# A step's fourth and fifth product exchanged, and the weight sets of the second layer re-timed, in a two-layer kernel planned at build time

## The chip, the core and the metric

The kernel runs on one core of one Trainium2 chip. The metric is the device time of one execution in microseconds (us). One more execution was recorded by the hardware profiler, and the views below are of that one.

## What is computed

The reference is a linear attention whose output feeds two dense feed-forward layers, all in fp32:

```
kv  = einsum('bhsd,bhse->bhde', k, v);  out = einsum('bhsd,bhde->bhse', q, kv)
a   = out / sqrt(mean(out*out, -1) + 1e-6) * g_norm          # 8 x 8 x 576 x 64
x   = a, heads side by side                                  # 4608 tokens x 512
x   = (s * relu(x @ w_in)**2 + b) @ w_out                    # first layer, 512 -> 2048 -> 512
out = silu(x @ w_in2) @ w_out2                               # second layer
```

## The kernel before

**Precision.** TensorE multiplies in a reduced fp32 form. Each fp32 factor is split into a rounded part and a rest, and each product is three matmuls (high by high, high by rest, rest by high), always 128x128 by 128x512.

**Stages.** The tokens are nine blocks of 512. The attention makes all blocks, and meanwhile the first layer works through blocks 0 to 4 one at a time, in 80 units (`unit`, 16 per block; the first matmuls stand at lines L210 to L212). Then come six pairs of blocks, 0 to 5 (`hidden`, `outputs`): pairs 0 and 1 are the first layer on the last four blocks, pairs 2 to 5 the second layer on eight blocks. One last block ends the second layer in units again.

**A pair's step.** A pair uses Strassen's scheme in Winograd's form, with seven products for eight. `hidden(tp, j)` is step j (of 8) of pair tp: the seven products B11, T2, T1, B21, T3, T4, B22 in that order, each in two halves of three matmuls (L964). They accumulate in three PSUM banks, X, Y and Z: `BANK = (X, Y, Z, X, Y, Y, Z)`. VectorE (DVE) takes the sums between them: `x1` copies X after B11; `u2` = Y + x1 is read after T2; `u3` = Y + x1 after T3; then `h22` = Z + u3. All of u2, u3 and h22 stand at L989. Three of them free a bank for a product: T3 may not start before u2 is read, T4 not before u3, B22 not before h22. `outputs` multiplies two finished steps by the second weight matrix (L1098 to L1100, six matmuls each), `total` takes each result from PSUM into a tile `ya`, and `results` adds those up on GpSimd (POOL, L1132) and stores them.

**Sets.** Each weight matrix of a layer is cut in 8 sets of two 128-row tiles; a set is turned into the 8 Winograd factors (`factors`) and stored in DRAM. There are 32 sets, 16 per layer. A set of the second layer is 4 loads, the decoding of a wide number format on ScalarE (ACT), DVE and POOL, 4 sums, 8 splits and 8 stores, about 60 short instructions on DVE, ACT, POOL and the DMA queue. Decoded tiles come from a pool of SBUF that is closed after the last set; only then are four more buffers for the pairs' inputs (`Q_RING`) and two for hidden values there (`turn3`).

**Order.** Nobody writes the order by hand. Every operation goes to `Plan.add` with a key, its needs, and a price per engine; `Plan.run` simulates the engines and emits each operation when and where it would start first, among equals the lowest key. What it emits is each engine's fixed order on the chip, and every engine works through its order strictly in turn. All DMAs are issued by SyncE (SP). The plan prices a DMA at 0.7 us to start, its transfer (0.73 us for 256 KB), and 1.1 us to end.

Of the kernel before, what the change touches and what calls it, by code (L numbers as in the profile page):

```python
# [19 lines left out]
class Plan:  # L20
# [112 lines left out]
def kernel(  # L133
# [237 lines left out]
    def factors(layer, kind, j, key, before):  # L371
        me = (layer, kind, j)
        begin = [started(key)] + (before or [("w", 0, k_, m, 1) for k_, m in late])
        b = [("rq", me + (n,)) for n in range(8)]
        w = lambda n: w32[b[n]][:, 1]
        full = lambda n: [("full", n) + me]
        for f in range(2):
            for c in range(2):
                n, m = quarter_of(kind, f, c), 2 * j + f
                if layer:  # L380
                    decode(1, kind, m, c, QW, "2", key + 0.2 * (2 * f + c), needs=begin, quarter=b[n], made=full(n))
# [499 lines left out]
    def pair_direct(tp):  # L881
# [16 lines left out]
        for kk in range(KH):  # L898
# [44 lines left out]
    def hidden(tp, j):  # L943
# [63 lines left out]
        S = lambda n: lambda: tmp[n, me]  # L1007
        add({ACT: 0.59, DVE: 0.69}, k(0), x1, needs=done(0), makes=[("x1",) + me], takes=[tb["x1"]])
        add({DVE: 0.69}, k(1), plus("u", Y, "x1"), needs=done(1) + [("x1",) + me], makes=[("u2",) + me], takes=[tb["u"]])
        add({DVE: 0.69}, k(4), plus("b", Y, "x1"), needs=done(4) + [("u2",) + me] + turn_, makes=[("u3",) + me], takes=[tb["b"]])  # L1010
        add({DVE: 0.69}, k(4) + 0.05, plus("b", Z, "b"), needs=done(2) + [("u3",) + me], makes=[("h22",) + me])
        add({DVE: 0.69}, k(5), add_up("c", B(Y), S("x1"), ALU.add), needs=done(5) + [("u3",) + me], makes=[("h21",) + me],
            gives=[tb["x1"]])
        add({DVE: 0.69}, k(6), add_up("a", B(Z), S("u"), ALU.add), needs=done(6) + [("h22",) + me], makes=[("h12",) + me],
            gives=[tb["u"]])

        for src, ready, kk in (("d", done(3) + [("x1",) + me], k(3)), ("b", [("h22",) + me], k(4) + 0.1),
                               ("c", [("h21",) + me], k(5) + 0.1), ("a", [("h12",) + me], k(6) + 0.1)):
            def curve(e, src=src):
# [334 lines left out]
```

## Time and profile before

| | us |
|---|---|
| median of 3 runs | 1608.47 (1605.17 to 1610.91) |
| the profiled execution, its own time | 1607.83 |
| its span, first to last instruction | 1606.1 |
| TensorE (PE) busy in the span | 1568.3 (98%) |
| VectorE (DVE) busy | 1069.5 (67%) |
| ScalarE (ACT) busy | 925.2 (58%) |
| GpSimd (POOL) busy | 627.0 (39%) |

Busy time is the union of an engine's instructions. A matmul's end is modelled and overlaps the next, so a stretch in which PE is fully busy says only that it never stood still. The number of matmuls that it began in a stretch tells more.

### The profile page before, as it was taken

The numbers are of one execution on the slowest core, as the hardware profiler recorded it, in microseconds if no ns is written. First come the engines' busy times: TensorE is split into PE (matmuls) and PEld (weight loads), VectorE is DVE, ScalarE is ACT, GpSimd is POOL, SyncE is SP. The second block draws the span as 40 slices with busy tenths as digits, with TensorE's granted clock in tenths as the row PEclk, the third lists the DMA queues.
The fourth block names the chain that finished last, engine by engine and source line by source line (L and its number), as shares of the span: only waits on it lengthen the run. The fifth ranks groups of instructions, "written<-read, shape, count | busy, mean of one in ns | idle before, by whom it ended". The sixth has DMA issues, their size and how long they took to land.

```text
span 1606.1 us, 23369 instructions
## 1 busy us (share of the span) xinstructions
PE 1568.3 (98%) x7393; PEld 1263.6 (79%) x7393; DVE 1069.5 (67%) x1944; ACT 925.2 (58%) x1791; POOL 627.0 (39%) x566
## 2 busy tenths in 40 slices
PE   8999999999999999999999999999999999999999
PEld 6777877877777777787788888888888788878887
DVE  6786777777776577988678746765667566656521
ACT  5896666666677677776667453544354445444222
POOL 1331111211225133457637752762266237622310
PEclk9999999999999999999999999999999999999999
DMA  9765687886666889888878786777687767876684
GB/s 217 187 177 149 209 262 238 253 236 207 194 221 210 281 274 301 290 259 276 276 243 260 254 267 192 242 213 233 187 285 197 238 190 239 198 230 192 206 205 140
DMA packets 354395, 366.49 MB, mean 228 GB/s; under 512 B 175712, under 2 KB 237152, under 8 KB 354272
## 3 DMA queue, kind: packets, MB, share of 16 engines
q1 hardware_dynamic: 354144, 365.00, 75.5%
q8 instruction: 59, 0.97, 0.2%
q14 instruction: 64, 0.52, 0.1%
q0 software_dynamic: 128, 0.00, 0.0%
HBM read 274.73 MB, written 90.18 MB: 227 GB/s over the span
## 4 chain that ended last, share of the span: by engine, by line
PE 49%; DMA 4%; DVE 2%; SPq 2%; POOL 1%; issue 1%; ACT 0%; DVEq 0%; POOLq 0%; ACTq 0%
PE hp L964 21%; PE acc L1098 8%; PE acc L1100 8%; PE acc L1099 7%; SPq L227 2%; DMA win<-wi 1%; PE acc L773 1%; PE acc L771 1%; PE acc L772 1%; PE h L210 1%; PE h L212 1%; PE h L211 1%; POOL ya L1132 1%; DMA xt_d<-ya 0%; DMA x<-x_d 0%
## 5 line engine op out<-in xcount | busy, mean ns | idle before, releaser
L964 PE MATMUL hp<-xo,win 128*128 128x512 f32 x2016 | 516.8, 393 | 12.8 <-DVE tmp L989 10.4
L964 PEld LDWEIGHTS hp<-xo,win 128*128 128x128 f32 x2016 | 378.7, 188 | 103.6 <-DVE tmp L989 15.1
L218 POOL TENSOR_TENSOR g<-tmp,g 128x512 fp32r<-128x512 f32 x192 | 249.8, 1304 | 358.2 <-ACT g L215 253.1
L1098 PE MATMUL acc<-g,wout 128*128 128x512 f32 x672 | 265.2, 395 | 2.1 <-DVE ya L224 1.3
L1107 DVE TENSOR_TENSOR ya<-acc,ya 128x512 f32<-128x512 f32 x252 | 172.2, 686 | 140.3 <-PE acc L1100 134.5
L1100 PE MATMUL acc<-g,wout 128*128 128x512 f32 x672 | 264.0, 393 | 0.0
L1099 PE MATMUL acc<-g,wout 128*128 128x512 f32 x672 | 263.3, 392 | 0.0
L1098 PEld LDWEIGHTS acc<-g,wout 128*128 128x128 f32 x672 | 126.4, 188 | 31.1 <-DVE ya L224 1.7
L1100 PEld LDWEIGHTS acc<-g,wout 128*128 128x128 f32 x672 | 126.5, 188 | 29.0
L1099 PEld LDWEIGHTS acc<-g,wout 128*128 128x128 f32 x672 | 126.4, 188 | 27.1 <-POOL g L218 0.2
L210 PE MATMUL acc<-gh,wo 128*128 128x512 f32 x320 | 133.6, 418 | 1.4 <-ACT gh L215 1.4
L215 ACT ACTIVATE g<-tmp 128x512 fp32r<-128x512 f32 x192 | 121.0, 630 | 24.1 <-DVE tmp L1003 16.3
L211 PE MATMUL acc<-gh,wo 128*128 128x512 f32 x320 | 127.4, 398 | 3.5 <-DVE gh L218 3.5
L210 PE MATMUL h<-xh,wi 128*128 128x512 f32 x320 | 126.8, 396 | 0.5 <-DVE gh L218 0.5
L212 PE MATMUL acc<-gh,wo 128*128 128x512 f32 x320 | 126.2, 394 | 0.1
L212 PE MATMUL h<-xh,wi 128*128 128x512 f32 x320 | 125.2, 391 | 0.0
L211 PE MATMUL h<-xl,wi 128*128 128x512 f32 x320 | 124.9, 390 | 0.0
L734 ACT ACTIVATE h<-h 128x512 f32<-128x512 f32 x96 | 55.9, 582 | 119.0 <-PE h L212 118.5
L215 ACT ACTIVATE g<-hp 128x512 fp32r<-128x512 f32 x144 | 85.9, 596 | 66.8 <-PE acc L1100 30.4
L989 DVE TENSOR_TENSOR tmp<-hp,tmp 128x512 f32<-128x512 f32 x144 | 98.6, 685 | 38.3 <-PE hp L964 35.5
L218 DVE TENSOR_TENSOR g<-hp,g 128x512 fp32r<-128x512 f32 x144 | 98.6, 685 | 34.7 <-ACT g L215 34.2
L1003 DVE TENSOR_TENSOR hp<-hp,tmp 128x512 f32<-128x512 f32 x144 | 99.6, 694 | 31.6 <-PE hp L964 30.9
(147 smaller groups left out, 2604.6 us busy)
## 6 DMA issues: line engine op xcount, KB each, us to landing
wout<-wo SPq DMA_DIRECT2D x368, 256.0 KB, 3.9
win<-wi SPq DMA_DIRECT2D x144, 512.0 KB, 5.0
wi<-rq SPq DMA_DIRECT2D x96, 256.0 KB, 3.2
wo<-rq SPq DMA_DIRECT2D x96, 256.0 KB, 3.5
win<-wi SPq DMA_DIRECT2D x80, 256.0 KB, 4.0
raw<-in_moe_w_out_dram SPq DMA_DIRECT2D x38, 256.0 KB, 4.4
raw<-in_moe_w_in_dram SPq DMA_DIRECT2D x34, 256.0 KB, 4.0
q<-in_q_dram SPq DMA_DIRECT2D x112, 72.0 KB, 2.9
```

What stands on the lines that cost most here:

```text
L210: nc.tensor.matmul(ps, wh, xh, start=first, stop=False)
L211: nc.tensor.matmul(ps, wh, xl, start=False, stop=False)
L212: nc.tensor.matmul(ps, wl, xh, start=False, stop=last)
L215: nc.scalar.activation(hi, src, AF.Copy)
L218: eng[e].tensor_tensor(lo, src, f32(hi), op=ALU.subtract)
L964: nc.tensor.matmul(to, w[:, wn, f_], x_[:, xn], start=first and n == 0, stop=kk == KH - 1 and n == 2, skip_group_check=True)
L989: nc.vector.tensor_tensor(t, bank[me, a], tmp[b_, me], op=ALU.add)
L1003: nc.vector.tensor_tensor(t, a(), b_(), op=op)
L1098: nc.tensor.matmul(to, w[:, 0, dd], gh, start=a == 0, stop=False)
L1099: nc.tensor.matmul(to, w[:, 0, dd], gl, start=False, stop=False)
L1100: nc.tensor.matmul(to, w[:, 1, dd], gh, start=False, stop=a == 1)
L1107: nc.vector.tensor_tensor(y2[tp, i, d], st["ps"], y2[tp, i, d], op=ALU.add)
```

## The change

Three things change. T3 and B21 change places in the order of the products (with the factors that they use, A12 and S3, which are stored in that order), so that T3 is the fourth product and B21 the fifth. The second layer's sets get other keys: 8 of them instead of 12 have keys ahead of the pairs, and those in the pairs get keys 6 units later. And after 100 us of planned time the plan prices a DMA's transfer 10% longer and its end at 1.6 us.

```
-    DMA_START, DMA_END = 0.7, 1.1
+    DMA_START, DMA_END, DMA_BUSY, BUSY_FROM, BUSY_RATE = 0.7, 1.1, 1.6, 100, 1.1
...
-                dma = max(dma, end + self.DMA_START) + op[8]
-                end = dma + self.DMA_END
+                busy = end > self.BUSY_FROM
+                dma = max(dma, end + self.DMA_START) + op[8] * (self.BUSY_RATE if busy else 1.0)
+                end = dma + (self.DMA_BUSY if busy else self.DMA_END)
...
-    A11, S2, S1, A12, S3, A22, S4, A21 = range(8)
+    A11, S2, S1, S3, A12, A22, S4, A21 = range(8)
...
+        late_key = key + (6 if key >= base(0) - 6 else 0)
...
-            k2 = key + 0.7 + 0.05 * n
+            k2 = late_key + 0.7 + 0.05 * n
...
-    B11, T2, T1, B21, T3, T4, B22 = range(7)
+    B11, T2, T1, T3, B21, T4, B22 = range(7)
...
-    BANK = (X, Y, Z, X, Y, Y, Z)
+    BANK = (X, Y, Z, Y, X, Y, Z)
...
-        read = {3: "x1", 4: "u2", 5: "u3", 6: "h22"}
+        read = {B21: "x1", T3: "u2", T4: "u3", B22: "h22"}
...
-        add({DVE: 0.69}, k(4), plus("b", Y, "x1"), needs=done(4) + [("u2",) + me] + turn_, makes=[("u3",) + me], takes=[tb["b"]])
+        add({DVE: 0.69}, k(T3), plus("b", Y, "x1"), needs=done(T3) + [("u2",) + me] + turn_, makes=[("u3",) + me], takes=[tb["b"]])
...
-        steps = ((0, KF + 3), (2 * NS, 48), (2 * NS + 12, base(0) - 6), (len(sets), base(NL1) + 8))
+        steps = ((0, KF + 3), (2 * NS, 44), (2 * NS + 8, base(0) - 6), (len(sets), base(NL1) + 8))
```

Since the plan is made anew, instructions move on every engine from about the 14th unit on. Three places follow; lines of the changed kernel are numbered up to two higher.

**PE, end of step 0 of pair 0.** In a name such as `xo31` the first digit is the product's place in the step, the second its half; `hp` is a bank, and `acc` belongs to the last unit. Before:

```order
L964 MATMUL hp_6440<-xo21_5810,win_5998 128x512 x3
L210 MATMUL acc_5644<-gh_6393,wo15_1833 128x512
L211 MATMUL acc_5644<-gh_6394,wo15_1833 128x512
L212 MATMUL acc_5644<-gh_6393,wo15_1833 128x512
L964 MATMUL hp_6375<-xo30_5756,win_5998 128x512 x3
L964 MATMUL hp_6375<-xo31_5863,win_5998 128x512 x3
L964 MATMUL hp_6404<-xo40_5779,win_6047 128x512 x3
L964 MATMUL hp_6404<-xo41_5877,win_6047 128x512 x3
L964 MATMUL hp_6404<-xo50_5915,win_6047 128x512 x3
L964 MATMUL hp_6404<-xo51_5964,win_6047 128x512 x3
L964 MATMUL hp_6440<-xo60_5953,win_6053 128x512 x3
```

And now:

```order
L966 MATMUL hp_6418<-xo21_5889,win_5993 128x512 x3
L211 MATMUL acc_5648<-gh_6372,wo15_1869 128x512
L212 MATMUL acc_5648<-gh_6373,wo15_1869 128x512
L213 MATMUL acc_5648<-gh_6372,wo15_1869 128x512
L966 MATMUL hp_6385<-xo30_5720,win_5993 128x512 x3
L966 MATMUL hp_6385<-xo31_5856,win_5993 128x512 x3
L966 MATMUL hp_6354<-xo40_5785,win_6047 128x512 x3
L966 MATMUL hp_6354<-xo41_5872,win_6047 128x512 x3
L966 MATMUL hp_6385<-xo50_6000,win_6047 128x512 x3
L966 MATMUL hp_6385<-xo51_6032,win_6047 128x512 x3
L966 MATMUL hp_6418<-xo60_6039,win_6054 128x512 x3
```

Before, the fifth and the sixth product (T3, T4) follow each other in bank Y (`hp_6404`); now B21's six matmuls in X (`hp_6354`) stand between them, and between T2 and T3 only T1 is left.

**DVE, the same step, from u2 (the first L989 row) to h22 (the last).** The rows between belong to sets, but for L224, which is a block's output. Before:

```order
L989 TENSOR_TENSOR tmp_6437<-hp_6404,tmp_6401 128x512
L320 TENSOR_SCALAR raw_6414<-raw_6414 128x256
L305 TENSOR_SCALAR raw_6414<-raw_6414 128x256
L320 TENSOR_SCALAR raw_6420<-raw_6420 128x256
...
L403 TENSOR_TENSOR rq_6479<-rq_6389,rq_6455 128x256
L403 TENSOR_TENSOR rq_6486<-rq_6479,rq_6384 128x256
L218 TENSOR_TENSOR rq_6455<-rq_6455 128x256
L218 TENSOR_TENSOR rq_6384<-rq_6384 128x256
L218 TENSOR_TENSOR rq_6479<-rq_6479 128x256
L218 TENSOR_TENSOR rq_6389<-rq_6389 128x256
L989 TENSOR_TENSOR tmp_6503<-hp_6404,tmp_6401 128x512
L989 TENSOR_TENSOR tmp_6503<-hp_6440,tmp_6503 128x512
```

And now:

```order
L991 TENSOR_TENSOR tmp_6415<-hp_6385,tmp_6382 128x512
L225 COPY y_6424<-acc_5616 128x512
L306 TENSOR_SCALAR raw_6380<-raw_6380 128x256
L321 TENSOR_SCALAR raw_6380<-raw_6380 128x256
L311 SCALAR_TENSOR_TENSOR raw_6380<-rq_6422,raw_6380 128x256
L321 TENSOR_SCALAR raw_6406<-raw_6406 128x256
L991 TENSOR_TENSOR tmp_6457<-hp_6385,tmp_6382 128x512
L306 TENSOR_SCALAR raw_6406<-raw_6406 128x256
L991 TENSOR_TENSOR tmp_6457<-hp_6418,tmp_6457 128x512
```

Twelve rows of a set stood between u2 and u3; now four do, and one output.

**SP, the loads of pair 4, step 3.** `win` is a load of first weights (the row of interest is its third group), `wout` one of second weights, `out` a store of pair 3's results. Before:

```order
L227 DMA out_0_dram<-ya_7056 32x16x32 x4
L227 DMA wout_12945<-wo2_0_103 128x512
L227 DMA wout_12945<-wo2_1_104 128x512
L227 DMA out_0_dram<-ya_6973 32x16x32 x4
L227 DMA win_12976<-wi2_3_98 128x1024
```

And now:

```order
L228 DMA win_12830<-wi2_3_98 128x1024
L228 DMA wout_12836<-wo2_0_103 128x512
L228 DMA wout_12836<-wo2_1_104 128x512
L228 DMA out_0_dram<-ya_6869 32x16x32 x4
L228 DMA win_12870<-wi2_3_98 128x1024
L228 DMA out_0_dram<-ya_6668 32x16x32 x4
```

The third group of `win` was issued behind all eight stores of the pair before it; now it is issued behind three. Pairs 3 and 5 show the same.

## Rows read from the trace of the kernel before

**Rows 1.** The page's first lines: span, and PE's busy time.

```profile
span 1606.1 us, 23369 instructions
PE 1568.3 (98%) x7393; PEld 1263.6 (79%) x7393; DVE 1069.5 (67%) x1944; ACT 925.2 (58%) x1791; POOL 627.0 (39%) x566
```

**Rows 2.** Windows: each engine's busy us (and instructions begun), clock, DMA share.

```profile
450.00:550.00 100.00, 95.93 (x412) 75.89 (x411) 68.56 (x140) 71.52 (x146) 34.85 (x38) 1.00 0.72 238
550.00:600.00 50.00, 45.88 (x189) 35.97 (x188) 36.37 (x86) 38.56 (x79) 14.65 (x17) 0.97 0.74 242
600.00:650.00 50.00, 47.62 (x204) 37.46 (x203) 38.36 (x83) 38.11 (x77) 18.25 (x19) 1.00 0.91 302
650.00:700.00 50.00, 48.48 (x211) 39.27 (x210) 45.03 (x85) 36.91 (x71) 21.60 (x21) 1.00 0.87 287
700.00:750.00 50.00, 47.40 (x199) 37.96 (x198) 40.96 (x70) 36.46 (x67) 33.82 (x29) 0.97 0.80 253
750.00:800.00 50.00, 47.67 (x207) 38.28 (x206) 33.31 (x49) 34.37 (x60) 38.88 (x31) 1.00 0.89 291
800.00:850.00 50.00, 49.62 (x218) 40.44 (x217) 36.34 (x66) 31.66 (x59) 20.64 (x21) 1.00 0.78 249
850.00:900.00 50.00, 49.94 (x219) 40.63 (x218) 43.27 (x63) 35.39 (x62) 38.41 (x29) 1.00 0.83 264
1300.00:1400.00 100.00, 100.00 (x437) 81.73 (x436) 66.97 (x104) 47.29 (x82) 60.90 (x48) 1.00 0.75 212
```

**Rows 3.** What PE waited for: us in total, times, longest.

```profile
PE hp L964 <- DVE tmp L989: 10.4, 9, 2.4
PE hp L964 <- DMA win<-wi: 1.7, 3, 0.7
```

**Rows 4.** Timeline of PE: four starts of T4, with the wait before each.

```profile
575.32 5.05 PE L964 MATMUL hp<-xo,win 128*128 128x512 f32 x14 [2.16 <-DVE tmp L989]
...
588.02 1.65 PE L964 MATMUL hp<-xo,win 128*128 128x512 f32 x6 [1.29 <-DVE tmp L989]
...
771.10 1.20 PE L964 MATMUL hp<-xo,win 128*128 128x512 f32 x4 [1.27 <-DVE tmp L989]
...
791.86 1.43 PE L964 MATMUL hp<-xo,win 128*128 128x512 f32 x5 [1.06 <-DVE tmp L989]
```

**Rows 5.** Timeline of DVE up to the u3 that the first of these waited for.

```profile
572.09 0.42 DVE L403 TENSOR_TENSOR rq<-rq 128x256 f32<-128x256 f32 x1 [0.78 <-POOL rq L324]
572.90 0.42 DVE L403 TENSOR_TENSOR rq<-rq 128x256 f32<-128x256 f32 x1 [0.38 <-DMA wo<-rq]
573.24 1.43 DVE L218 TENSOR_TENSOR rq<-rq 128x256 fp32r<-128x256 f32 x4
574.58 1.41 DVE L989 TENSOR_TENSOR tmp<-hp,tmp 128x512 f32<-128x512 f32 x2
```

**Rows 6.** Windows behind two of PE's waits: the clock stands before the DMA share.

```profile
575.40:578.80 3.40, 3.40 (x8) 2.65 (x9) 1.61 (x3) 2.67 (x5) 1.56 (x2) 0.51 1.01 377
725.60:729.00 3.40, 3.40 (x10) 2.66 (x9) 2.71 (x6) 1.96 (x5) 2.66 (x3) 0.50 0.58 192
```

**Rows 7.** Timeline of PE: the last start before, and T3 of pair 1, step 0.

```profile
718.76 3.83 PE L964 MATMUL hp<-xo,win 128*128 128x512 f32 x15
725.02 1.16 PE L964 MATMUL hp<-xo,win 128*128 128x512 f32 x3 [2.43 <-DVE tmp L989]
```

**Rows 8.** Timeline of DVE: first and last of nine instructions ahead of that T3's u2, and u2.

```profile
719.15 0.68 DVE L1107 TENSOR_TENSOR ya<-acc,ya 128x512 f32<-128x512 f32 x1
...
723.69 0.69 DVE L1003 TENSOR_TENSOR hp<-hp,tmp 128x512 f32<-128x512 f32 x1
724.29 0.68 DVE L989 TENSOR_TENSOR tmp<-hp,tmp 128x512 f32<-128x512 f32 x1
```

**Rows 9.** DVE's sums of inputs in 565 to 900: ns, minimum, median, maximum.

```profile
L907 DVE TENSOR_TENSOR x<-x x6: 676/1026/1673, 711.2 to 877.4; 128x512 f32<-128x512 f32 x6
```

**Rows 10.** Timeline of PE: two waits in a run of outputs.

```profile
627.53 0.50 PE L1098 MATMUL acc<-g,wout 128*128 128x512 f32 x1 [1.27 <-DVE ya L224]
...
629.73 0.51 PE L1098 MATMUL acc<-g,wout 128*128 128x512 f32 x1 [0.54 <-ACT ya L222]
```

**Rows 11.** DMA issues in 700 to 870: KB each, median us to landing.

```profile
wout<-wo SPq DMA_DIRECT2D x59, 256.0 KB, 4.6
xt_d<-ya SPq DMA_DIRECT2D x8, 256.0 KB, 7.0
raw<-in_moe_w_out_dram SPq DMA_DIRECT2D x4, 256.0 KB, 4.5
```

**Rows 12.** Timeline of DVE: a copy held up by a store, and the u3 behind it.

```profile
790.52 0.69 DVE L224 COPY ya<-acc 128x512 f32<-128x512 f32 x1 [1.75 <-DMA xt_d<-ya]
791.12 0.68 DVE L989 TENSOR_TENSOR tmp<-hp,tmp 128x512 f32<-128x512 f32 x1
```

**Rows 13.** Pair 3, step 5: PE's row of T2's second half, and DVE up to u2.

```profile
1129.96 1.55 PE L964 MATMUL hp<-xo,win 128*128 128x512 f32 x6
...
1130.74 0.69 DVE L218 TENSOR_TENSOR g<-hp,g 128x512 fp32r<-128x512 f32 x1 [0.66 <-ACT g L215]
1131.35 0.69 DVE L1003 TENSOR_TENSOR hp<-hp,tmp 128x512 f32<-128x512 f32 x1
1131.95 0.68 DVE L1107 TENSOR_TENSOR ya<-acc,ya 128x512 f32<-128x512 f32 x1
1132.54 0.68 DVE L989 TENSOR_TENSOR tmp<-hp,tmp 128x512 f32<-128x512 f32 x1
```

More of the change, by code (lines that the diff above doesn't have):

```diff
@@ L380, in factors @@
                 if layer:
-                    decode(1, kind, m, c, QW, "2", key + 0.2 * (2 * f + c), needs=begin, quarter=b[n], made=full(n))
+                    decode(1, kind, m, c, QW, "2", late_key + 0.2 * (2 * f + c), needs=begin, quarter=b[n], made=full(n))
                     continue
@@ L392, in spill @@
                     dma(w_d[0, kind, j][:, n], f32(w_t[kind, 0, m])[:, :, cs])
-                add(both(QW), key + 0.05 * (2 * f + c), recover, needs=ready + begin, makes=full(n), takes=[b[n]],
+                add(both(QW), late_key + 0.05 * (2 * f + c), recover, needs=ready + begin, makes=full(n), takes=[b[n]],
                     gives=lent_to[f"w{kind}{m}"])
                 if n != A21:
-                    add({"SP": 0.48}, key + 0.4 + 0.05 * (2 * f + c), spill, needs=full(n), makes=[("wd", n) + me],
+                    add({"SP": 0.48}, late_key + 0.4 + 0.05 * (2 * f + c), spill, needs=full(n), makes=[("wd", n) + me],
                         gives=lent_to[f"w{kind}{m}"], move=0.73)
@@ L403, in go @@
                 eng[e].tensor_tensor(w(o), w(x), w(y), op=op)
-            add(both(QW), key + 0.6 + 0.01 * o, go, needs=full(x) + full(y), makes=full(o), takes=[b[o]],
+            add(both(QW), late_key + 0.6 + 0.01 * o, go, needs=full(x) + full(y), makes=full(o), takes=[b[o]],
                 gives=[] if layer else [b[n] for n in (x, y) if n not in (S1, S2)])
@@ L907, in go @@
                     eng[e].tensor_tensor(tile_[dst, kk], tile_[a, kk], tile_[b_, kk], op=op)
-                at = {T3: -3, T1: -2.5, T2: 4 / 7 * 0.8 - 1.2, T4: 4 / 7 * 3.8 - 1.2}[o]
+                at = {T3: -3, T1: -2.5, T2: 4 / 7 * 0.8 - 1.2, T4: 4 / 7 * 4.8 - 1.2}[o]
                 add(both(T), base(tp) + at + 0.3 * kk, go, needs=needs, makes=[sx(o)], gives=[x[n, kk] for n in gives])
@@ L1007, in hidden @@
         S = lambda n: lambda: tmp[n, me]
-        add({ACT: 0.59, DVE: 0.69}, k(0), x1, needs=done(0), makes=[("x1",) + me], takes=[tb["x1"]])
-        add({DVE: 0.69}, k(1), plus("u", Y, "x1"), needs=done(1) + [("x1",) + me], makes=[("u2",) + me], takes=[tb["u"]])
-        add({DVE: 0.69}, k(4), plus("b", Y, "x1"), needs=done(4) + [("u2",) + me] + turn_, makes=[("u3",) + me], takes=[tb["b"]])
-        add({DVE: 0.69}, k(4) + 0.05, plus("b", Z, "b"), needs=done(2) + [("u3",) + me], makes=[("h22",) + me])
-        add({DVE: 0.69}, k(5), add_up("c", B(Y), S("x1"), ALU.add), needs=done(5) + [("u3",) + me], makes=[("h21",) + me],
+        add({ACT: 0.59, DVE: 0.69}, k(B11), x1, needs=done(B11), makes=[("x1",) + me], takes=[tb["x1"]])
+        add({DVE: 0.69}, k(T2), plus("u", Y, "x1"), needs=done(T2) + [("x1",) + me], makes=[("u2",) + me], takes=[tb["u"]])
+        add({DVE: 0.69}, k(T3), plus("b", Y, "x1"), needs=done(T3) + [("u2",) + me] + turn_, makes=[("u3",) + me], takes=[tb["b"]])
+        add({DVE: 0.69}, k(T3) + 0.05, plus("b", Z, "b"), needs=done(T1) + [("u3",) + me], makes=[("h22",) + me])
+        add({DVE: 0.69}, k(T4), add_up("c", B(Y), S("x1"), ALU.add), needs=done(T4) + [("u3",) + me], makes=[("h21",) + me],
             gives=[tb["x1"]])
-        add({DVE: 0.69}, k(6), add_up("a", B(Z), S("u"), ALU.add), needs=done(6) + [("h22",) + me], makes=[("h12",) + me],
+        add({DVE: 0.69}, k(B22), add_up("a", B(Z), S("u"), ALU.add), needs=done(B22) + [("h22",) + me], makes=[("h12",) + me],
             gives=[tb["u"]])
-        for src, ready, kk in (("d", done(3) + [("x1",) + me], k(3)), ("b", [("h22",) + me], k(4) + 0.1),
-                               ("c", [("h21",) + me], k(5) + 0.1), ("a", [("h12",) + me], k(6) + 0.1)):
+        for src, ready, kk in (("d", done(B21) + [("x1",) + me], k(B21)), ("b", [("h22",) + me], k(T3) + 0.1),
+                               ("c", [("h21",) + me], k(T4) + 0.1), ("a", [("h12",) + me], k(B22) + 0.1)):
             def curve(e, src=src):
@@ L1042, in hidden @@
         for i, src, ready, kk, gives in (
-            (B11, "d", sg("d"), k(3) + 0.1, []), (B22, "b", sg("b"), k(4) + 0.2, []), (B21, "c", sg("c"), k(5) + 0.2, []),
+            (B11, "d", sg("d"), k(B21) + 0.1, []), (B22, "b", sg("b"), k(T3) + 0.2, []), (B21, "c", sg("c"), k(5) + 0.2, []),
             (T1, "e", sg("e"), kt + 0.03, [tb["e"]]), (T3, "a2", sg("a2"), kt + 0.05, []), (T2, "f", sg("f"), kt + 0.07, []),
```

## The prediction

> **What bounds the kernel now.** The page's first lines come first: PE is busy for 1568.3 of 1606.1 us, far ahead of DVE [rows 1]. So only a moment in which PE stands still, or runs below full speed, can be given back. How much that is at which stage is read from the windows, by counting matmuls: a fully fed stretch, 1300 to 1400, begins 437 in 100 us, that is 0.2288 us each [rows 2]. The six windows from 550 to 850, which hold the last units of the first layer and pairs 0 and 1, begin 189 + 204 + 211 + 199 + 207 + 218 = 1228, where 1311 fit: 83 x 0.2288 = 19.0 us are lost there. The window 450 to 550 begins 412 and loses 25 x 0.2288 = 5.7 us. From 850 on little is lost (219 of 218.5 in the next window). In both stretches DVE and ACT work on the second layer's sets beside the units and pairs.
>
> Next the list of waits: PE's waits at L964 on a `tmp` of L989 are 10.4 us in 9, and loads of `win` make it wait 1.7 us [rows 3]. The timeline of PE gives the places. Four starts of T4 wait 2.16, 1.29, 1.27 and 1.06 us [rows 4]; T3 of pair 1, step 0, waits 2.43 [rows 7]; two starts in a run of outputs wait 1.27 and 0.54 [rows 10]. Then DVE's timeline up to the value waited for: the u3 of the first T4 stands behind seven short instructions of sets, two of which wait themselves, for POOL and for a store [rows 5]; the u2 of the T3 stands behind nine instructions that run almost without a gap from 719.15 to 724.29 [rows 8]. A late u3 hits PE at once, since T4 follows T3 in the same bank with nothing of the step between. Last, the clock: right after the two long waits the granted clock is 0.51 and 0.50 for 3.4 us, the lower of the two levels (1.2 of 2.4 GHz) [rows 6]. At half speed 3.4 us do the work of 1.7, so each of these waits costs 1.7 us more.
>
> **The change part by part.** Gains first, then new waits.
>
> *T4 behind B21 instead of T3.* Six matmuls, 6 x 0.2288 = 1.37 us, now lie between T3's end and T4, and u3 can be taken in them. That covers the waits of 1.29, 1.27 and 1.06 by itself; even a copy held up 1.75 us by a store, after which the last of these came [rows 12], is then hidden. It covers 2.16 only to 0.8, but there the order also shows four set rows and one output ahead of u3 in place of twelve set rows. I take all: 2.16 + 1.29 + 1.27 + 1.06 = 5.8, and the first one's dip, 1.7: **7.5 removed**. Bound: the first keeps 0.8 us and its dip, 5.0.
>
> *T3 of pair 1, step 0.* The nine instructions ahead of u2 thin out, as outputs and sets are spread differently, and 2.43 + 1.7 = 4.1 go. But T3 now has only T1, 1.37 us, behind T2, and in the new order a sum of inputs stands right ahead of u2. Such a sum takes 0.68 to 1.67 us, 1.03 in the median [rows 9]; with one of 1.4 the sum is 0.21 for PE's end to be seen + 1.4 + 0.69 for u2 + 0.06 to release PE = 2.36, and 2.36 - 1.37 = 1.0 stays: **3.1 removed** (bounds 4.1, and nothing if the queue is as full as before).
>
> *The run of outputs.* 1.27 + 0.54: **1.8 removed**, since products of the next step now stand between them (bound nothing).
>
> *The rest of that stage.* 19.0 - 7.5 - 4.1 - 1.8 = 5.6 us are short waits on sets and their buffers. Fewer sets fall in the last units, but the work is only moved. I take half, **2.8 removed** (0 to 5.6).
>
> *450 to 550.* The 5.7 us lie where sets are made between units. About 3.5 sets end there now instead of about 5, by the order, so 5.7 x 1.5 / 5 = **1.7 removed** (0 to 5.7). The first layer's sets come up to four units earlier; nothing waits there in either list, so 0.
>
> *Loads of `win` in step 3 of pairs 3 to 5.* Issued ahead of five stores instead of behind all eight: **1.7 removed** [rows 3] (bound nothing).
>
> *The price of a DMA.* It costs no instruction. A 256 KB load is now planned to land after 0.7 + 0.73 x 1.1 + 1.6 = 3.1 us instead of 2.5. The trace says 4.5 and 4.6 for loads, and 7.0 for the stores `xt_d` that free a `ya` [rows 11]. So instructions that need a DMA are put later, though still earlier than it lands. By the Trainium skill ("DMA: Bandwidth & Descriptors", section "Anatomy of one DMA — SWDGE (gpsimd) path") a transfer, on GpSimd's path, takes about 2.0 us and its bytes over 436e9 a second, an estimate of 2.6 us for 256 KB. By that the new price would be long enough, and the 2.6 us of stores below would fall away; this trace, whose issues are SP's, disagrees [rows 11].
>
> *New waits, outputs.* In steps 4 of pairs 1 and 2 the new order has bunches of four to seven outputs, each of which needs a `ya`, and a `ya` is free when its store has landed: 7.0 us against 3.1 planned, 3.9 late at most. Before, such a copy waited 1.75 [rows 12]. I take 1.3 on PE each, like the 1.27 of [rows 10]: **2.6 added** (0 to 7.8).
>
> *New wait, start of pair 2.* Sets end later, so the four input buffers and two hidden ones opened behind them come in pair 2, step 2, instead of pair 1, step 6. Sums of inputs for pair 2, and ten outputs in step 0, meet POOL's share of the last sets. I take **2.0 added** (from nothing to 2.43 + 1.7 = 4.1, as at the worst start above). By the Trainium skill ("SBUF — State Buffer", section "SBUF: two separate sides") DVE with two SBUF operands and GpSimd share a pair of ports, and one waits for the whole instruction of the other. That speaks against more such work at a pair's start; the spread of 676 to 1673 ns for one form agrees [rows 9].
>
> *T3's halved cover.* In pairs 0 and 1, with irregular work on DVE, T3 has one product less behind T2 in all 16 steps. Three waits of 0.5 us, as the shortest of [rows 10]: **1.5 added** (0 to 16 x 0.5 = 8). In the second layer's steady steps it is closer: T2's second half begins at 1129.96, and u2, third of a run that starts when ACT's value comes, ends at 1132.54 + 0.68 = 1133.22, that is 3.26 later [rows 13]. T3 is now due 15 matmuls behind that half's start, 15 x 0.2288 = 3.43 us. Less 0.05 until PE goes on (724.29 + 0.68 to 725.02 [rows 7, 8]) 0.12 us are spare; cost 0. Without that cover it costs PE the whole excess in each of some 40 steps.
>
> Sum: 7.5 + 3.1 + 1.8 + 2.8 + 1.7 + 1.7 = 18.6 removed, 2.6 + 2.0 + 1.5 = 6.1 added, 12.5 net. The profiled execution took 1607.8, so 1595.3; it lies 0.6 below the median of the runs, so for a median **1596 us**.
>
> **The rivals.**
> *Nearly all goes.* The 5.6 and 5.7 leave too, and of the new waits only 2 to 4 us stay: 7.5 + 3.1 + 1.8 + 5.6 + 4 + 1.7 = 23.7, less 3, is 20.7: about **1587**. For it speaks that DVE is busy only 67% [rows 1]; against it that sets must still be made beside the pairs.
> *The sets are only pushed back.* The bunches wait their full 7.8, pair 2's start 4.1: 18.6 - 7.8 - 4.1 - 1.5 = 5.2, about **1603**. For it speaks the 7.0 [rows 11], against it that PE has hidden products planned between most outputs.
> *DVE's queue is as bad as before.* DMAs still land later than planned, so the head of DVE's queue waits [rows 5, 12] and only T4's 5.0 and the 1.7 of `win` go, with 4 us of new waits: 2.7, about **1605**, no measurable change.
> *u2 is not in time.* If one more DVE instruction (0.60 from start to start [rows 13]) gets ahead of u2 in the steady steps, T3 waits 0.60 - 0.12 = 0.48, 40 times, 19 us: 1595.9 + 19 = about **1615**, slower. It decides from 12.5 / 40 + 0.12 = 0.43 us of lateness in each step. Against it: the same three instructions stand ahead of u2, in the same sequence.
>
> **How the numbers follow.** Forecast (1590 to 1601) 0.52; nearly all 0.14; pushed back 0.14; queue as bad 0.11; u2 late 0.09. A change of 0.3%, 4.8 us, is about what a measurement of this kernel can tell, so 1603.6 to 1613.3 counts as the same: the queue case, half of pushed back and 0.02 of u2 late, 0.20. Slower is the rest of u2 late, 0.07; faster is what remains, 0.73. The range reaches from below the first rival, 1585, to just above the queue case, 1607; it leaves out u2 late and tails.
>
> **What would show it.** Right, if the windows from 550 to 850 begin some 1260 matmuls instead of 1228, no T4 waits over 0.3 us on L991, and the clock stays at 1.00 there but for pair 1's or pair 2's start. Each step by itself: `win` no longer among PE's waits; PE waiting on `ya` or `acc` in steps 4; L991 with small waits at T3 in pairs 0 and 1. Wrong, if T3 waits some tenths of a us in every second-layer step, or if PE's loss moves to 850 to 950, where it lost nothing.

## The result, and the profile after

The changed kernel takes 1588.68 us (median of 4 runs, 1588.18 to 1589.46); the kernel before took 1606.82 over 4 (one more than in the table above). The ratio is 0.9887, 95% interval 0.9860 to 0.9914: 18 us faster, and the span of the profiled execution fell by 18.8, from 1606.1 to 1587.3. The forecast was 1596, range 1585 to 1607.

The first lines of the page after, against [rows 1]:

```profile
span 1587.3 us, 23243 instructions
PE 1558.8 (98%) x7393; PEld 1263.9 (80%) x7393; DVE 1075.8 (68%) x1937; ACT 914.3 (58%) x1779; POOL 641.6 (40%) x585
```

PE has the same 7393 matmuls, and stood still less. Where, the windows tell, columns as in [rows 2]:

```profile
450.00:550.00 100.00, 99.11 (x434) 80.55 (x433) 63.96 (x133) 71.72 (x147) 32.69 (x34) 1.00 0.73 242
550.00:600.00 50.00, 46.88 (x198) 38.05 (x197) 33.44 (x63) 38.34 (x75) 18.70 (x19) 0.97 0.71 225
600.00:650.00 50.00, 50.00 (x221) 41.16 (x220) 41.23 (x73) 32.81 (x65) 20.73 (x22) 1.00 0.87 284
650.00:700.00 50.00, 50.00 (x220) 41.10 (x219) 41.54 (x68) 38.45 (x74) 31.13 (x29) 1.00 0.84 264
700.00:750.00 50.00, 49.06 (x214) 39.70 (x213) 42.29 (x71) 34.99 (x66) 39.84 (x34) 1.00 0.84 272
750.00:800.00 50.00, 44.91 (x187) 35.78 (x187) 37.38 (x64) 31.78 (x60) 31.45 (x28) 0.97 0.89 291
800.00:850.00 50.00, 50.00 (x221) 41.14 (x220) 41.43 (x76) 34.52 (x67) 25.77 (x26) 1.00 0.85 278
```

From 550 to 850 there are 1261 matmuls instead of 1228, and 450 to 550 has 434 instead of 412. But these windows don't show all of it: the same clock time is now about 11 us further on in the program. So the starts of the same matmul in both traces are compared:

| first matmul of | before, us | after, us | gained in the part up to it |
|---|---|---|---|
| pair 0 (attention and units done) | 561.2 | 550.4 | 10.8 |
| pair 2 (pairs 0 and 1 done) | 873.9 | 855.8 | 7.2 |
| pair 3 (pair 2 done) | 1028.2 | 1012.3 | -2.1 |
| the last units | 1493.7 | 1475.0 | 2.8 |

More than half of the gain came before pair 0, where the prediction had looked at 450 to 550 only. One window over the units shows it, first before, then after:

```profile
200.00:450.00 250.00, 244.13 (x1372) 194.83 (x1371) 179.47 (x405) 162.35 (x368) 45.10 (x60) 1.00 0.79 235
```

```profile
200.00:450.00 250.00, 249.08 (x1401) 200.46 (x1400) 187.85 (x428) 167.82 (x376) 51.10 (x67) 1.00 0.78 236
```

PE stood still for 5.9 us there and now does for 0.9. The waits of DVE in 195 to 450, again before and after, say what came in time:

```profile
DVE raw L320 <- DMA raw<-in_moe_w_in_dram: 7.2, 7, 2.3
DVE raw L320 <- DMA raw<-in_moe_w_out_dram: 5.0, 6, 1.8
```

```profile
DVE raw L321 <- DMA raw<-in_moe_w_out_dram: 1.5, 1, 1.5
DVE raw L321 <- DMA raw<-in_moe_w_in_dram: 1.2, 1, 1.2
```

`raw` is a set's tile as loaded. DVE stood with a decoding instruction at the head of its queue until the load had landed, 12.2 us in all; now 2.7. The list of PE's waits, against [rows 3], has these:

```profile
PE acc L1100 <- DVE ya L225: 5.0, 2, 3.6
PE hp L966 <- DVE g L219: 3.1, 1, 3.1
PE acc L1100 <- DVE ya L1109: 1.5, 2, 0.9
PE hp L966 <- DVE tmp L991: 0.9, 2, 0.6
```

The waits for a `tmp` fell from 10.4 to 0.9 and those for `win` are gone, but two of over 3 us are new. Behind both, the granted clock (it stands before the DMA share) is at the lower of its two levels for 3.4 us:

```profile
580.20:583.60 3.40, 3.40 (x10) 2.65 (x9) 2.47 (x5) 2.73 (x6) 0.86 (x2) 0.50 0.37 104
757.70:761.10 3.40, 3.40 (x10) 2.62 (x9) 0.76 (x2) 3.40 (x8) 2.71 (x3) 0.50 0.73 172
```

So the two falls of the clock that [rows 6] showed have not gone: there are two again, behind other waits. The first of these waits is at T2 of step 2 of pair 0:

```profile
579.06 3.26 PE L966 MATMUL hp<-xo,win 128*128 128x512 f32 x9 [3.12 <-DVE g L219]
```

T2 needs bank Y, which the step before gives back with its last `g`. Before, it waited 0.42 us there, after T4 had waited 2.16 and 1.29 in steps 0 and 1. Counted by matmuls, these three steps lost 6.5 us before and lose 5.0 now: most of what T4 lost there has moved, and has not gone.

The wait at 757 is worth following. PE's row, then DVE's timeline up to the `ya` that it waited for, then POOL's:

```profile
756.82 0.50 PE L1100 MATMUL acc<-g,wout 128*128 128x512 f32 x1 [3.62 <-DVE ya L225]
```

```profile
745.75 1.26 DVE L405 TENSOR_TENSOR rq<-rq 128x256 f32<-128x256 f32 x1
747.01 0.69 DVE L219 TENSOR_TENSOR g<-hp,g 128x512 fp32r<-128x512 f32 x1
747.62 0.83 DVE L405 TENSOR_TENSOR rq<-rq 128x256 f32<-128x256 f32 x1
748.37 7.20 DVE L219 TENSOR_TENSOR rq<-rq 128x256 fp32r<-128x256 f32 x5
755.49 0.69 DVE L1005 TENSOR_TENSOR hp<-hp,tmp 128x512 f32<-128x512 f32 x1
756.09 0.68 DVE L225 COPY ya<-acc 128x512 f32<-128x512 f32 x1
```

```profile
745.43 9.86 POOL L1134 TENSOR_TENSOR ya<-ya 128x512 f32<-128x512 f32 x7
```

Five splits of a set take 7.20 us, 1.43 us from start to start, where a split of this form takes 0.42 (the median of 34 from 600 on). Beside them POOL sums pair 0's results, seven in 9.86 us, 1.40 us from start to start, where the first alone takes 1.29. Both go forward in the same steps: they take turns. The `g` of 747.01, which has only one operand in SBUF (`hp` is a bank), takes its usual 0.69 us beside the same sums. The kernel before has such slow sums and splits too, 6 of over 0.9 us between 680 and 800, against 9 now.

### The profile page after: what moved, and what is told of

Same layout as the page of the kernel before. It is cut to its first block, busy times and chain, and to the rows that moved or that the text cites. A ratio compares the mean times of both kernels' runs of the same rounds, so it can differ in the third digit from the quotient of the medians.

```text
span 1587.3 us, 23243 instructions
## 1 busy us (share of the span) xinstructions
PE 1558.8 (98%) x7393; PEld 1263.9 (80%) x7393; DVE 1075.8 (68%) x1937; ACT 914.3 (58%) x1779; POOL 641.6 (40%) x585
## 4 chain that ended last, share of the span: by engine, by line
PE 49%; DVE 2%; ACT 1%; POOL 1%; DMA 1%; issue 1%; ACTq 0%; POOLq 0%; DVEq 0%
PE hp L966 21%; PE acc L1100 8%; PE acc L1102 7%; PE acc L1101 7%; PE acc L775 1%; PE acc L773 1%; PE acc L774 1%; PE h L211 1%; PE h L213 1%; PE h L212 1%; DVE rq L219 1%; DMA wo<-rq 0%; DMA x<-y 0%; ACT g L216 0%; POOL g L219 0%
## 5 line engine op out<-in xcount | busy, mean ns | idle before, releaser
L1134 POOL TENSOR_TENSOR ya<-ya 128x512 f32<-128x512 f32 x84 | 109.0, 1324 | 46.4 <-DVE ya L1109 37.0
L325 POOL TENSOR_TENSOR rq<-raw 128x256 uint32<-128x256 uint32 x72 | 45.6, 633 | 184.0 <-DVE raw L311 109.2
```

What stands on the lines that cost most here:

```text
L1134: eng[e].tensor_tensor(y2[tp, i, d], y2[tp, i, d], y2[tp, j, d], op=ALU.add)
```

## The experiments

Six kernels make the three edits singly and in twos; with before and after they are all eight combinations. Two change a number, one adds work, three are aimed at what the trace after showed. "Ratio" is to the kernel before on the same chip; the stages are from the profiled executions (start of pair 0; pairs 0 and 1; pair 2; pairs 3 to 5). The rest, 112.3 to 112.4 us, is the same in all of them. The profiled execution of the exchange alone lay 4.4 us above its median, that of the keys alone 4.9, that without keys 3.5 below; of the rest none was off by more than 2.5.

| kernel | ratio (95%) | median us | to pair 0 | pairs 0, 1 | pair 2 | 3 to 5 |
|---|---|---|---|---|---|---|
| before | | | 561.2 | 312.6 | 154.4 | 465.5 |
| exchange (e1) | 1.0004 (0.9988 to 1.0019) | 1610.2 | 564.9 | 318.3 | 154.4 | 462.9 |
| keys (e2) | 1.0013 (0.9996 to 1.0031) | 1612.2 | 567.3 | 314.2 | 156.3 | 465.4 |
| price (e3) | 1.0034 (1.0019 to 1.0049) | 1614.4 | 553.9 | 328.9 | 154.2 | 465.3 |
| keys, price (e4) | 0.9957 (0.9943 to 0.9971) | 1602.4 | 550.9 | 309.1 | 160.6 | 466.7 |
| exchange, keys (e5) | 0.9990 (0.9974 to 1.0007) | 1604.1 | 560.5 | 310.1 | 155.0 | 462.7 |
| exchange, price (e6) | 0.9968 (0.9955 to 0.9981) | 1601.2 | 548.4 | 318.5 | 154.2 | 462.6 |
| all three | 0.9887 (0.9860 to 0.9914) | 1588.7 | 550.4 | 305.4 | 156.5 | 462.7 |
| price 1.5 (e7) | 0.9901 (0.9880 to 0.9922) | 1590.5 | 550.9 | 309.6 | 154.3 | 462.7 |
| price 3.5 late (e8) | 0.9903 (0.9883 to 0.9923) | 1589.7 | 551.3 | 308.0 | 154.7 | 463.0 |
| u2 later (e9) | 0.9948 (0.9934 to 0.9962) | 1597.8 | 550.3 | 304.7 | 156.1 | 471.5 |
| sets on POOL (e10) | 0.9859 (0.9842 to 0.9876) | 1584.5 | 552.6 | 300.7 | 155.1 | 462.8 |
| keys 12 (e11) | 0.9829 (0.9816 to 0.9842) | 1578.5 | 550.5 | 296.8 | 155.2 | 462.4 |
| both (e12) | 0.9843 (0.9828 to 0.9857) | 1580.0 | 552.3 | 297.9 | 155.7 | 462.5 |

**e1, the exchange alone**, on the kernel before:

```
-    BANK = (X, Y, Z, X, Y, Y, Z)
+    BANK = (X, Y, Z, Y, X, Y, Z)
```

> Only the exchange of T3 and B21; keys of the sets and price of a DMA as before. Theory (each edit works in its own stage): the units keep their time, so pair 0 starts within 2 us of 561.2; T4 no longer waits for a tmp over 0.5 us; 6 to 9 us are gained in pairs 0 and 1: 1598 to 1601 us. Rival (the gain is not the exchange, the sets' keys made DVE's queue short): T4's waits become waits for other DVE results, 1604 to 1608 us.

Nothing was gained, and T4 still waits. Counting what PE loses right ahead of a T4 (its start less the start of the matmul before it and 0.23 us for that one, where over 0.25 us), before loses 6.9 us in 5 places, this kernel 6.4 in 5. The largest wait is another one, at the T2 of step 2 named above, for a DVE result as the rival said: PE's row, then the heads of ACT's and DVE's queues shortly before.

```profile
600.20 2.93 PE L964 MATMUL hp<-xo,win 128*128 128x512 f32 x6 [8.52 <-DVE g L218]
```

```profile
591.67 0.44 ACT L301 ACTIVATE rq<-raw 128x256 f32<-128x256 f32 x1 [2.25 <-DMA wo<-rq]
```

```profile
591.61 0.30 DVE L320 TENSOR_SCALAR raw<-raw 128x256 uint32<-128x256 uint32 x1 [1.92 <-DMA raw<-in_moe_w_in_dram]
```

DVE and ACT stood before a late transfer for 1.92 and 2.25 us. That is only a part of the 8.52: the changed kernel waits 3.12 at the same T2, and the rest was not followed. No kernel without the exchange waits more than 0.42 us there; of those with it, e5 alone doesn't. So this wait comes with the exchange, though not in every plan. A cover of six matmuls (1.37 us) is not enough for T4 either.

**e2, the keys alone:**

```
+        late_key = key + (6 if key >= base(0) - 6 else 0)
...
-        steps = ((0, KF + 3), (2 * NS, 48), (2 * NS + 12, base(0) - 6), (len(sets), base(NL1) + 8))
+        steps = ((0, KF + 3), (2 * NS, 44), (2 * NS + 8, base(0) - 6), (len(sets), base(NL1) + 8))
```

> Only the sets' keys (8 ahead of the pairs, 6 units later in them). Theory: pair 0 starts 2 to 4 us earlier, T4 behind T3 still waits, some of it in other steps: 1603 to 1608 us. Rival (the keys are what counts): DVE has no bunch of set rows ahead of u3, the four waits of T4 fall under 0.5 us each, 1597 to 1601 us.

No gain, and pair 0 starts 6 us later: the theory was wrong on the units, and the rival on T4, which loses 9.5 us.

**e3, the price alone:**

```
-    DMA_START, DMA_END = 0.7, 1.1
+    DMA_START, DMA_END, DMA_BUSY, BUSY_FROM, BUSY_RATE = 0.7, 1.1, 1.6, 100, 1.1
```

> Only the longer price of a DMA after 100 us of plan. Theory (formed on the changed kernel's trace, where pair 0 starts 10.8 us earlier and DVE's waits for raw loads between 195 and 450 us fall from 12.2 to 2.7 us): pair 0 starts 7 to 11 us earlier, DVE waits under 4 us for raw there, 1597 to 1601 us. Rival (units gained by the keys of the first layer's sets, or by nothing but another plan): pair 0 starts within 3 us of before, 1604 to 1609 us.

Pair 0 starts 7.3 us earlier, as expected, though DVE's waits for `raw` between 195 and 450 fall to 8.7 us only (7.3 and 1.4). The sum came as neither expected: 16.3 us are lost again in pairs 0 and 1. The largest wait, SP's row, ACT's and PE's:

```profile
788.38 5.50 SPq L228 DMA_DIRECT2D xt_d<-ya  x8
```

```profile
794.08 1.87 ACT L223 COPY ya<-acc 128x512 f32<-128x512 f32 x3 [8.63 <-DMA xt_d<-ya]
```

```profile
794.72 0.80 PE L1099 MATMUL acc<-g,wout 128*128 128x512 f32 x1 [10.80 <-ACT ya L223]
```

Here is the late store of a `ya` that the prediction had priced at 1.3 us, with 10.8. ACT began to wait at 785.45. For 2.9 us of its wait the store had not been issued; SP issued five stores of sets just before it. The rest, 5.7 us, is its way to landing.

**e4, the change without the exchange** (the edits of e2 and e3 on the kernel before; one line by which it differs from the changed one):

```
-    B11, T2, T1, T3, B21, T4, B22 = range(7)
+    B11, T2, T1, B21, T3, T4, B22 = range(7)
```

> The change without the exchange: new keys and the new price. Theory: units as in the changed kernel (pair 0 starts near 550), but T4 directly behind T3 waits again, 5 to 9 us in pairs 0 and 1: 1594 to 1598 us. Rival (with good keys and price the order of products is of no account): 1588 to 1591 us.

7 us faster than before, 11 slower than the changed kernel, more than expected. T4 loses 8.1 us, but in pairs 0 and 1 only 3.1, less than the theory's 5 to 9; there the largest waits are two for a `ya` (4.17 and 3.32). The worst T4 is in pair 2:

```profile
933.79 1.65 PE L966 MATMUL hp<-xo,win 128*128 128x512 f32 x3 [4.85 <-DVE tmp L991]
```

and `win` is late again (3.6 us). So the exchange is worth nothing by itself and 11 us on top of the other two.

**e5, the change without the price** (the edits of e1 and e2; against the changed kernel):

```
-                end = dma + (self.DMA_BUSY if busy else self.DMA_END)
+                end = dma + self.DMA_END
```

> Exchange and keys, without the longer price. New theory (late DMAs hold the heads of DVE's, ACT's and POOL's queues; the exchange gives cover only where the queue moves on): the queues' heads wait for raw loads again (12 us on DVE between 195 and 450), pair 0 starts within 4 us of before, single waits of 4 us and more stay in pairs 0 and 1: 1603 to 1611 us. Rival (exchange and keys together are what brings the gain, as each frees DVE's queue for the other): 1592 to 1599 us.

As the theory expected: pair 0 at 560.5, a single wait of 8.0 us. But DVE's waits for `raw` between 195 and 450 are 5.4 us, not 12, and the wait of 8.0 is no late load. DVE, then POOL, then PE:

```profile
754.26 11.92 DVE L404 TENSOR_TENSOR rq<-rq 128x256 f32<-128x256 f32 x1 [2.21 <-DMA wi<-rq]
766.10 0.68 DVE L218 TENSOR_TENSOR g<-hp,g 128x512 fp32r<-128x512 f32 x1
766.71 0.41 DVE L404 TENSOR_TENSOR rq<-rq 128x256 f32<-128x256 f32 x1
```

```profile
751.01 10.01 POOL L1133 TENSOR_TENSOR ya<-ya 128x512 f32<-128x512 f32 x8
760.96 4.93 POOL L1152 TENSOR_TENSOR ya<-ya 128x512 f32<-128x512 f32 x4
```

```profile
766.84 1.65 PE L965 MATMUL hp<-xo,win 128*128 128x512 f32 x3 [7.97 <-DVE g L218]
```

One DVE sum, 0.41 us when it is alone, lasts 11.92 us, until POOL's run of twelve sums is over.

**e6, the change without the keys** (the edits of e1 and e3; against the changed kernel, some of its lines):

```
-        late_key = key + (6 if key >= base(0) - 6 else 0)
...
-            k2 = late_key + 0.7 + 0.05 * n
+            k2 = key + 0.7 + 0.05 * n
...
-        steps = ((0, KF + 3), (2 * NS, 44), (2 * NS + 8, base(0) - 6), (len(sets), base(NL1) + 8))
+        steps = ((0, KF + 3), (2 * NS, 48), (2 * NS + 12, base(0) - 6), (len(sets), base(NL1) + 8))
```

> Exchange and price, the sets' keys as before. New theory: pair 0 starts 6 to 8 us earlier than before as with the price alone, and with cover and with loads in time the waits of pairs 0 and 1 shrink: 1592 to 1600 us. Rival (any one edit left out loses all, the changed kernel is one lucky plan among many): 1604 to 1612 us.

Between the two: 5 us faster than before. The units are the fastest of all (548.4), pairs 0 and 1 take 318.5, and T4 loses 10.6 us there. Of these 5.8 stand at a T4 that waits for its input (`xo`, from ACT) and not for u3:

```profile
730.73 0.79 PE L965 MATMUL hp<-xo,win 128*128 128x512 f32 x1 [5.64 <-ACT xo L216]
```

**e7, another price:**

```
-    DMA_START, DMA_END, DMA_BUSY, BUSY_FROM, BUSY_RATE = 0.7, 1.1, 1.6, 100, 1.1
+    DMA_START, DMA_END, DMA_BUSY, BUSY_FROM, BUSY_RATE = 0.7, 1.1, 1.5, 100, 1.1
```

> The changed kernel with an end price of 1.5 us instead of 1.6, a difference without a meaning of its own. New theory: 1586 to 1594 us. Rival (luck of a plan): anywhere up to 1606 us, with single waits of 4 us and more at other places than in the changed kernel.

The gain stays, though the waits stand elsewhere. One of 5.0 us at a T4 is new, and DVE's row ahead of the u3 that it needed shows the turns with POOL again, four splits in 5.72 us (T4 starts at 752.32, as u3 ends behind them):

```profile
745.95 5.72 DVE L219 TENSOR_TENSOR rq<-rq 128x256 fp32r<-128x256 f32 x4
```

With e8 and e10 to e12 there are five more plans with all three edits, at ratios of 0.983 to 0.990: it is no single lucky plan.

**e8, a price as long as the trace's landings in the pairs:**

```
-                end = dma + (self.DMA_BUSY if busy else self.DMA_END)
+                end = dma + (3.5 if late else self.DMA_BUSY if busy else self.DMA_END)
```

(`late` holds from 540 us of plan on.)

> The changed kernel with the end priced at 3.5 us for a DMA issued after 540 us of plan, so that 256 KB are planned to land after 5.0 us where the trace shows 4.2 to 6.6. New theory: POOL and the copies into ya no longer wait over 2 us for stores in pairs 0 to 2, and 3 to 7 us of the changed kernel's waits there go: 1582 to 1586 us. Rival (the longer price only pushes sets and sums back): 1588 to 1600 us.

A miss. The waits for transfers did go: POOL's for `y<-ya`, between 545 and 960, fell from 8.8 us in the changed kernel to 2.4. The time did not, since PE still waits for a `ya`, 4.0 and 2.7 us. So the waits that are left in pair 1 are not POOL's waits for transfers.

**e9, u2 made later** in pairs 3 to 5, all else in the same order:

```
+                if o == "u" and tp >= 3:
+                    copy(DVE, t, bank[me, a])
                 nc.vector.tensor_tensor(t, bank[me, a], tmp[b_, me], op=ALU.add)
```

> The changed kernel, same order on all engines, with one more DVE copy (0.60 us) that the plan doesn't know ahead of u2 in all 24 steps of pairs 3 to 5; its result is overwritten. Theory (u2 is just in time in half of the steps: in the changed kernel's trace 12 of the 24 have 0.08 to 0.21 us between u2's end and T3's start, the others 0.67 to 1.87): T3 waits about 0.5 us in those 12 and not in the others, 6 us more than the changed kernel, 1594 to 1597 us. Rival 1 (as the prediction priced it, every step loses 0.48): 24 x 0.48 = 11.5 more, 1600 us. Rival 2 (DVE catches up, nothing waits): 1588 to 1590 us.

The median is 1597.8, just above the theory's range; the span of the profiled execution is 1595.0, 7.7 us above the changed kernel's. DVE's rows of one step and PE's T3:

```profile
1115.62 0.68 DVE L1111 TENSOR_TENSOR ya<-acc,ya 128x512 f32<-128x512 f32 x1
1116.22 0.68 DVE L225 COPY tmp<-hp 128x512 f32<-128x512 f32 x1
1116.94 0.69 DVE L993 TENSOR_TENSOR tmp<-hp,tmp 128x512 f32<-128x512 f32 x1
```

```profile
1117.68 0.96 PE L966 MATMUL hp<-xo,win 128*128 128x512 f32 x3 [0.42 <-DVE tmp L993]
```

The copy makes u2 0.72 us later, not 0.60; u2 writes the same tile, but that this is the reason is not shown. T3 starts 0.57 to 0.70 us later in the same 12 steps, and at most 0.1 in the others: 7.5 us in all.

**e10, the sets' sums and splits on POOL alone in the pairs:**

```
+        set_on = {POOL: both(QW)[POOL]} if late_key > key else both(QW)
...
-            add(both(QW), late_key + 0.6 + 0.01 * o, go, needs=full(x) + full(y), makes=full(o), takes=[b[o]],
+            add(set_on, late_key + 0.6 + 0.01 * o, go, needs=full(x) + full(y), makes=full(o), takes=[b[o]],
```

(and the same for the splits)

> The changed kernel with the sums and splits of the sets that have keys in the pairs on POOL alone (before: DVE or POOL, as the plan finds). Theory (DVE's splits of 128x256 take 1.5 instead of 0.42 us beside POOL's sums of ya, and this makes PE wait 3.8 us for a ya at 757 of the changed kernel): no DVE instruction of that form over 0.5 us from 600 us on, no wait over 2 us for a DVE ya, 1580 to 1586 us. Rival (the work only queues up on POOL, whose splits of hidden values come late instead): waits for POOL or for tmp of 3 us and more, 1590 to 1600 us.

As expected, 4 us faster than the changed kernel by the medians, though the two intervals overlap; in the profile pairs 0 and 1 take 4.7 us less. PE's list has no wait for a `ya` over 1.6 us:

```profile
PE hp L967 <- DVE g L219: 4.1, 3, 3.1
...
PE acc L1101 <- DVE ya L225: 1.6, 1, 1.6
```

**e11, keys 12 units later:**

```
-        late_key = key + (6 if key >= base(0) - 6 else 0)
+        late_key = key + (12 if key >= base(0) - 6 else 0)
```

> The changed kernel with keys 12 units later in the pairs instead of 6. Theory (the keys' worth lies in pairs 0 and 1, where they thin out the sets; pair 2 pays for it): pairs 0 and 1 take up to 3 us less than in the changed kernel, pair 2 some 2 to 6 more, 1588 to 1594 us. Rival (the later the sets the better): 1580 to 1586 us.

The rival was right in kind, and the gain is larger than it said: 1578.5 us, the fastest kernel here. Pairs 0 and 1 take 296.8 us, 8.6 less than in the changed kernel, and pair 2 pays nothing for it. DVE's slow splits and sums of sets (over 0.9 us, from 500 us on) fall from 19 to 10, and none is left between 680 and 800.

**e12, e10 and e11 together** (both diffs):

> Keys 12 units later and the sets' sums and splits in the pairs on POOL alone, both on the changed kernel. Theory (both take away the same wait, DVE's slow splits beside POOL's sums in pair 1; keys 12 already leave none of them between 680 and 800 us): little on top of the later keys, 1576 to 1580 us. Rival (two different gains, 4 and 10 us, that add up): 1573 to 1575 us. Rival 2 (POOL has the sets in pair 2 as well as its sums of inputs there): 1582 us and more.

1580.0, nothing on top of e11: both take the same wait away, as the theory said.

## Why the prediction was right, and by how much it was off

The direction and the range held. The sum was short, 12.5 us against 18, and its terms lie in other places than the gain: 1.7 was priced ahead of pair 0, where 10.8 came, and 12.4 in pairs 0 and 1, where 7.2 came. That errors of opposite sign met within 8 us of the forecast is in part luck; the time is nearer to the rival "nearly all goes" (1587), which had a chance of 0.14. Of the signs, the 1261 matmuls came and T4's waits went, but the clock did not stay at 1.00: it fell behind the waits at 579 and 757.

**The step that failed: what the longer price is worth.** "The price of a DMA ... costs no instruction" led to no term at all, and "nothing waits there in either list, so 0" was said of units that no window had been shown of. With 1.7 us for 450 to 550 the units were priced at 1.7; they gave 10.8, of which that window alone gave 22 matmuls, 5.0 us. The four kernels with the price start pair 0 at 548 to 554, the four without at 560.5 to 567: it is the price, with any of the other edits (7 to 17 us in the four comparisons that differ by it alone). A set's load was planned to land after 2.5 us and takes 3.6 to 3.9 in this stage (the medians for `raw` from 195 to 450). So decoding stood ahead of its data in DVE's and ACT's order, and what PE waits for stood behind it. DVE's waits up to 450 do not show this by themselves: they are short in e2 and e5 too (3.9 and 5.4 us), which start pair 0 late. What goes with its start is DVE's and ACT's waits for `raw` together, from 195 us to pair 0: 50 us before and 47, 38 and 29 in e1, e2 and e5, against 14, 10, 11 and 4 in e3, e4, e6 and the changed kernel (the order is not strict: e7, with a price of 1.5, has 23 and starts pair 0 at 550.9). PE's own waits there are 9.3 to 10.8 us without the price and 1.4 to 4.3 with it. Which of PE's waits goes back to which load was not followed. The prediction had the numbers for it [rows 11], and used them only against the change.

**T4 behind T3: the waits right, the clock and the condition wrong.** Of the 7.5 us expected 5.8 were waits, and T4 loses 0.8 now instead of 6.9. The 1.7 for the clock did not come, since the wait of 3.12 at T2 took the place of T4's first two and the clock fell behind it. And "that covers the waits of 1.29, 1.27 and 1.06 by itself" fell in e1 (6.4 left) and e6 (4.8 left, without the late input). Only with the new keys does T4 lose little: 1.6 in e5, 0.8 with all three. The thinner order, which the prediction named as a help for the first of the four, is half of the mechanism for all; e7's 5.0 shows that one bunch of splits still undoes it.

**T3 of pair 1, and the run of outputs.** The 2.43 us are gone, and no new wait of 1.0 came in their place; of the 1.5 for T3's halved cover 0.5 came. In the run of outputs 1.8 was to go and 2.6 to come: what PE loses ahead of outputs in pairs 0 and 1, counted as for T4, rose from 2.6 to 6.1 us, 3.5 more instead of 0.8. The place was right, pair 1, the mechanism in the changed kernel was not: it is no store that lands late, it is DVE in turns with POOL (748 to 755). The Trainium skill ("SBUF — State Buffer", section "SBUF: two separate sides") says that DVE with two SBUF operands and GpSimd hold a shared pair of ports one at a time, for a whole instruction. The prediction cited this for the start of pair 2, where it gave 2.0 us; the trace agrees with it in the five splits, each of which lasts as long as one of POOL's sums. e5's 11.92 us beside twelve sums goes beyond one instruction. e10 shows that it was this: with the set work off DVE no such sum or split over 0.5 us is left from 600 us on, the wait of 3.6 us goes, and pairs 0 and 1 are 4.7 us shorter. Pairs 0 and 1 together were priced at 12.4 gained (7.5 + 3.1 + 1.8 + 2.8 - 1.3 - 1.5) and gave 7.2.

**Pair 2** was priced at 3.3 lost (2.0 and 1.3) and lost 2.1. **Loads of `win`**: 1.7 priced, 2.8 gained, and by the exchange alone: pairs 3 to 5 take 462.4 to 463.0 in every kernel with it, 465.3 to 466.7 without.

**u2 in time.** Read from the trace before as 3.26 us behind the start of T2's second half with T3 due at 3.43, it is 3.27 to 3.32 and 3.40 to 3.48 in the 12 tight steps of the changed kernel, and T3 never waits there. The rival's mechanism is real (e9), but it holds in 12 of the 24 steps of pairs 3 to 5, where the prediction counted every step, some 40 of them: e9 lost 7.5 us there, with 0.57 to 0.70 in each of the 12.

**How the edits work together.** By ratios, at 1607 us: exchange +0.6, keys +2.1, price +5.5, all three -18. Price and keys together give -6.9, exchange and price -5.1, exchange and keys -1.6. e7, a change of one number without a meaning, moved the total by some 2 us, so this is more than the scatter of plans. What the runs show is that the price gains in the units and, alone, loses it in pairs 0 and 1; that the keys take it out of there (with keys those two pairs take 305 to 314, without 313 to 329; with 12 units instead of 6, 297); and that the exchange needs a DVE that isn't held up. Windows over pairs 0 and 1 say what the price alone costs there and what the later keys bring; before, changed, e3, e11:

```profile
561.20:873.90 312.70, 299.55 (x1277) 240.23 (x1276) 242.71 (x444) 228.32 (x429) 163.14 (x146) 0.99 0.85 274
```

```profile
550.40:855.80 305.40, 296.24 (x1276) 241.42 (x1275) 241.58 (x418) 215.69 (x411) 170.30 (x156) 0.99 0.83 270
```

```profile
553.90:882.80 328.90, 303.30 (x1277) 243.74 (x1276) 258.37 (x448) 232.21 (x439) 183.68 (x174) 0.96 0.83 269
```

```profile
550.50:847.40 296.90, 292.37 (x1277) 239.15 (x1276) 226.42 (x397) 213.94 (x405) 172.90 (x159) 1.00 0.83 270
```

In e3 PE stands still for 25.6 us instead of 13.2. Three waits are most of it: the store's 10.80, 5.29 for a u3 and 2.62 for an `xo`. The remaining 4 us go with the clock, which is at 0.50 for 23.9 us instead of 6.8, in a part of which PE stands still anyway. Why the last two of these waits arise was not followed. In e11 PE stands still for 4.5 us instead of the changed kernel's 9.2, and the clock does not fall at all, which gives back 3.4 (two falls of 1.7). One of the two is hardly the keys' doing: e11 has the same wait of 3.12 at 579, and the clock happened to stay up behind it. That later keys help by taking set work away from POOL's sums of results is shown for the wait at 757 and the fall behind it, some 5 us; for the rest of their 10 us it is argued.

## What to carry to other kernels

Where every engine works strictly in order, a transfer planned to land too early holds the head of a queue, and all that stands behind it; here 0.6 us of price a load went with 7 to 17 us in one stage. So compare planned and measured landing stage by stage before looking at the busy shares. Edits to such a plan are not to be priced one by one: here each alone was worth nothing or less. When a wait goes, look whether it came back at another instruction, and whether the clock fell behind that one. And look in the trace for one form of instruction with several durations; in DVE's timeline 0.42 and 1.5 us for the same split showed in one line what no list of waits named.

## What was not expected of the hardware

A DVE sum of 128x256 with both operands in SBUF waited 11.92 us beside twelve of POOL's sums without a gap between them (1.27 to 1.32 us each); in the changed kernel five such splits took turns with POOL's, one for one. What decides between the two was not tried. And the spread: the changed kernel's four runs, few as they are, lie within 1.3 us, while the 32 of the kernel before that stood beside e1 to e4 on one chip range from 1603.2 to 1618.5.
